# Five pieces for the last weight, and its late sums as two halves of 144 columns in two PSUM banks

## The chip, the cores and the metric

The kernel runs on one core of a Trainium2 chip. The metric is device time in microseconds (us). The kernel before took 215.35 us, the median of three runs (215.19 to 215.35). A core has a matrix engine (PE, with its weight loads shown apart as PEld), a vector engine (DVE), a scalar engine (ACT), a general engine (POOL), a queue engine (SP) and 16 DMA engines. Each engine works through its own list of instructions in order; they meet at semaphores. Matrix products arrive in PSUM (eight banks), from where DVE or ACT copy them to SBUF; DMA moves data between SBUF and the main memory.

## The reference

For four rows `x` of 576 numbers, the output is `x + A + B`, after a first layer norm `xn = layernorm(x)`:

- A is attention over a cache: `q` from `layernorm`ed rows and `wq` (32 heads of 128), keys and values the last 2,048 of 8,192 cached positions of 16 key heads (each serves two query heads), softmax, and the result times `wo` (4096 x 576).
- B is a small mixer: a layer norm, `w1` and a gelu, a shift of four column groups, `w2`, a residual sum, then a layer norm, `w3` (576 x 4608), a gelu and `w4` (4608 x 576).

In short:

```python
xn = layernorm(x)
return x + attention(xn, k_cache[-2048:], v_cache[-2048:], wq) @ wo + mixer(xn, w1, w2, w3, w4)
# the last step inside mixer:  x1 + gelu(layernorm(x1) @ w3) @ w4
```

All inputs and the output are bf16. The output has only 4 rows, so nearly the whole time is spent reading 88.5 MB of cache and weights once.

## The kernel before

Everything that is read comes through one queue, SP's, in a fixed order: `wq`, `w1`, `w2`, `w3`, sixteen pieces of keys (2 MB each), sixteen of values, `wo` in between, and last `w4`. Each operation of every engine is recorded with a sort key by `add` and `add_dma`; an engine's list is its operations sorted by that key, and `waits` names the operations or transfers that must have ended.

The mixer's work up to the gelu behind `w3` is done early, while the keys arrive; its result stands in `h2T_sb` (36 blocks `t` of 128 rows by 4). Then a loop of four rounds transposes keys and makes scores, the softmax follows, and a second loop of four rounds (L429) multiplies the values as they arrive. Then comes the tail that this change is about:

- `pe_turn` and `pe_AO` (L446) multiply the attention result with `wo`, 64 matmuls of 288 columns. `acc_mm` (L444) sends them to four sums `ACC[0..3]`, each of 4 rows and 288 columns: sums 0 and 1 are the two halves of the 576 output columns for even blocks, 2 and 3 the same halves for odd blocks. Sum `k` stands on partitions 32k to 32k+3 and is made by column group `k` of the PE array, so that neighbouring matmuls run side by side. The sums are in banks 0, 1, 2 and 2. Before that, the residual `t1` is put into sums 0 and 1 (`pe_t1`).
- `w4` comes in four pieces given by `W4P`: blocks 0-13, 14-27, 28-33 and 34-35, into the space of the values, so each piece waits for the last loop round that reads that space. The third and the fourth are issued together, after the same wait. The products of blocks 0-13 (`MO0`) go to all four sums.
- The fold: ACT copies sums 2 and 3 from PSUM to SBUF as fp32 (L533), and PE adds them to sums 0 and 1 with two matmuls by a 4 x 4 identity (`pe_fold`, L525).
- Blocks 14-33 (`MO1`, `MO2`) use sums 0 and 1 only, two matmuls of 288 columns per block.
- The last piece is split by output half: the two matmuls of half 0 (`MOl0`), then those of half 1 (`MOl1`). DVE copies half 0 (L550) and ACT copies half 1 (L551), and each half goes out by its own DMA, from SP and from ACT (issued in L177), each waiting for its own copy.

```python
W4P = ((0, 14), (14, 28), (28, 34), (34, 36))
ACC = [ps[32 * k:32 * k + B, min(k, 2), 0:HALF] for k in range(4)]
a = 2 * (t % 2) + h if t < FOLD else h
```

Of the kernel before, what the change touches and what calls it, by code (L numbers as in the profile page):

```python
# [5 lines left out]
FP32 = mybir.dt.float32  # L6
BF16 = mybir.dt.bfloat16
ACTF = mybir.ActivationFunctionType
ALU = mybir.AluOpType
# [10 lines left out]
WO_AFTER = 3  # L20
V0_AFTER = 8
FOLD = 14
W4P = ((0, 14), (14, 28), (28, 34), (34, 36))


class Op:
# [12 lines left out]
def bass_parallel_sum__sliding_block_cached__mixer_s_mlp__decode_kernel(  # L39
    nc, A_x, A_k_cache, A_v_cache, A_wq, A_wo, B_x, B_w1, B_w2, B_w3, B_w4, out  # L40
):
    B, Sq, D = A_x.shape
# [11 lines left out]
    HALF = D // 2  # L54
    FH = F // 2
    RT = F // 128
# [3 lines left out]
    o2 = out.rearrange("b s d -> (b s) d")  # L60

    with ExitStack() as ctx:
        def sb(name, shape, dt):
            return ctx.enter_context(nc.sbuf_tensor(name, shape, dt))
# [43 lines left out]
        h2T_sb = sb("h2T_sb", [128, RT, 32], BF16)  # L108
# [7 lines left out]
        ident_f = sb("ident_f", [128, 128], FP32)  # L116
# [13 lines left out]
        OTx = PTb[:, 1024:1536].rearrange("p (b h q) -> p b h q", b=B, q=4)  # L130
        qmask = sb("qmask", [128, 4], FP32)
        sel32 = sb("sel32", [128, 32], BF16)
        ORT = sb("ORT", [128, 128], BF16)
        t1 = sb("t1", [B, D], FP32)
        fold_sb = P_sb[:, 0:2 * HALF].bitcast(FP32)
        out_t = sb("out_sb", [32 + B, HALF], BF16)
        out_sb = [out_t[32 * h:32 * h + B, :] for h in range(2)]

        ps = ctx.enter_context(nc.psum_tensor("ps", [128, 8, 512], FP32))[:]
        Sps = ps[:, 0:4, :]  # L140
        tb = [ps[:, 4 + k, :].bitcast(BF16).rearrange("p (t d) -> p t d", t=8) for k in range(NTB)]
        ACC = [ps[32 * k:32 * k + B, min(k, 2), 0:HALF] for k in range(4)]
        rinvps = ps[:, 3, 0:128]
        ORps = ps[:, 3, 128:256]
        OTps = lambda g: ps[:, 4 + g % 4, 0:8]
# [20 lines left out]
        def add(engine, emit, waits=(), sig=None, key=0.0, loop=None):  # L166
            seqc[0] += 1
            prog[engine].append(Op(emit, waits, sig, key, seqc[0], loop))

        def add_dma(pairs, skey, waits=(), key=0.0, engine="sp"):  # L170
            if skey not in S:
                S[skey] = sem("s_" + "_".join(str(k) for k in (skey if isinstance(skey, tuple) else (skey,))))
            dma_count[skey] = dma_count.get(skey, 0) + 16 * len(pairs)

            def emit(e):
                for o_, i_ in pairs:
                    e.dma_start(o_, i_).then_inc(S[skey], 16)  # L177
            add(engine, emit, waits, None, key)
            return ("dma", skey, dma_count[skey])
# [6 lines left out]
        KT = KV + G + 8.0  # L186
# [13 lines left out]
        def first_counts(e):  # L200
# [5 lines left out]
          waits=["ident_bf"], sig="perm_k", key=-95.5)  # L206
        P(lambda e: e.tensor_copy(out=perm_p[:].rearrange("p (i b) -> p i b", b=B), in_=ident_bf[:].rearrange("p (b i) -> p i b", b=B)),
          waits=["ident_bf"], sig="perm_p", key=-95)
# [8 lines left out]
        ev_wq, ev_w3, ev_k, ev_v, ev_w4 = [], [], [], [], []  # L217
# [27 lines left out]
        w4_sb = vring_t[:, 0:RT * D].rearrange("p (t n) -> p t n", n=D)  # L245
        for n, (t0, t1_) in enumerate(W4P):
            lst = (t1_ * D - 1) // UE
            ev_w4.append(add_dma([(w4_sb[:, t0:t1_, :], w4_src[:, t0:t1_, :])], ("w4", n),
                                 [f"PV{max(g for g in range(G) if g % NVS == lst)}"], KS + G + 0.1 * n))
        ev_o = [None, None]  # L250
        for h, eng in ((0, "sp"), (1, "act")):
            ev_o[h] = add_dma([(o2[:, HALF * h:HALF * (h + 1)], out_sb[h])], ("out", h),
                              [f"fin{h}"], 10000, engine=eng)
            add(eng, lambda e: None, [ev_o[h]], None, 10001)


# [58 lines left out]
        for j in range(4):  # L315
            add("dve", lambda e, j=j: e.tensor_copy(out=qp_out[:, j, :, :, 0:2], in_=qp_in[:, j, :, 0:B, :]),
                waits=["qTp", "qpad_zero"], sig="qT" if j == 3 else f"qT{j}", key=-25 + 0.1 * j)
# [39 lines left out]
        for n in range(NHB):  # L357
            p = n % 32
# [3 lines left out]
            eng, f = evac(n)  # L362
            add(eng, f, waits=[f"T{n}"] + ([f"SC{n // 8 - 2}"] if n >= 8 else []), sig=("eb", p), key=n + 0.2)
        for g in range(-1, G):
            s_ = g % 4
            if g < G - 1:
                add("pe", pe_SC(g), waits=[("L", ("eb", 8 * s_ + 6), 1), ("L", ("eb", 8 * s_ + 7), 1), ("L", ("qs", s_), 1)], sig=f"SC{g}",
                    key=(g + 1) // 4 + 0.01 * (8 * ((g + 1) % 4) + 1) + 0.005, loop=("k", (g + 1) // 4))
            else:
                add("pe", pe_SC(g), waits=[("c", ("eb", 30), NIT + 1), ("c", ("eb", 31), NIT + 1), ("c", ("qs", 3), NIT + 1)],  # L370
                    sig=f"SC{g}", key=NIT + 0.5)
        for g in range(G):
            P(lambda e, g=g: e.tensor_copy(out=Qs[:, g % 4], in_=Qpad[:, g]), waits=(["qT"] if g == 0 else []) + ([f"SC{g - 4}"] if g >= 3 else []),  # L373
              sig=("qs", g % 4), key=8 * g)
# [4 lines left out]
            waits=["rmax"], sig="negb", key=KS + 0.05)  # L379
        for q in range(4):  # L380
# [3 lines left out]
                waits=["negb"], sig=f"exp{q}", key=KS + 0.1 + 0.01 * q)  # L384
            add("dve", lambda e, cs=cs: e.transpose(PTb[:, cs], P_sb[:, cs]), waits=[f"exp{q}"], sig=f"PTb{q}", key=KS + 0.2 + 0.01 * q)  # L385
            add("pe", lambda e, q=q, cs=cs: e.matmul(ps[:, q, :], lhsT=perm_p[:], rhs=PTb[:, cs], start=True, stop=True),  # L386
                waits=[f"PTb{q}"] + (["perm_p"] if q == 0 else []), sig=f"PTp{q}", key=KS + 0.2 + 0.01 * q)
            dst = PTs[:, 16 * q:16 * q + 16, :].rearrange("p t r -> p (t r)")
            if q % 2 == 1:
                add("act", lambda e, q=q, dst=dst: e.activation(out=dst, in_=ps[:, q, :], func=ACTF.Copy), waits=[f"PTp{q}"],  # L390
                    sig=f"PTs{q}", key=KS + 0.3 + 0.01 * q)
            else:
                add("dve", lambda e, q=q, dst=dst: e.tensor_copy(out=dst, in_=ps[:, q, :]), waits=[f"PTp{q}"],  # L393
                    sig=f"PTs{q}", key=KS + 0.3 + 0.01 * q)
        for g in range(G):
            add("dve", lambda e, g=g: e.tensor_tensor(  # L396
                out=PTg[:, g % NPG], in0=PTs[:, :, 2 * g:2 * g + 2].unsqueeze(2).to_broadcast([128, NT, B, 2]),
                in1=bmask[:].unsqueeze(1).to_broadcast([128, NT, B, 2]), op=ALU.mult),
                waits=[f"PTs{q}" for q in range(4)] + ["bmask"] if g < NPG else [f"PV{g - NPG}"], sig=("pg", g % NPG),
                key=KS + 0.4 + 0.01 * g if g < NPG else KV + g - NPG + 0.6)  # L400
# [3 lines left out]
            waits=["rinv", "ident_f"], sig="diag", key=KS + 0.37)  # L404
        add("dve", lambda e: e.tensor_reduce(out=bmask[:, :, 0], in_=ident_bf[:].rearrange("p (i b) -> p b i", b=B), axis=AX.X, op=ALU.add),
            waits=["ident_bf"], sig="bmask0", key=-41)
        add("dve", lambda e: e.tensor_copy(out=bmask[:, :, 1], in_=bmask[:, :, 0]), waits=["bmask0"], sig="bmask", key=-40.9)
        add("pe", lambda e: e.matmul(rinvps, lhsT=ones_f[:], rhs=diag[:], start=True, stop=True), waits=["diag", "ones_f", "PTs3"],  # L408
            sig="rinvp", key=KS + 0.6)
        add("dve", lambda e: e.tensor_tensor(  # L410
            out=rinvM.rearrange("p b h q -> p (b h) q"),
            in0=rinvps.unsqueeze(2).to_broadcast([128, 128, 4]),
            in1=qmask[:].unsqueeze(1).to_broadcast([128, 128, 4]), op=ALU.mult),
            waits=["rinvp", "qmask"], sig="rinvM", key=KS + 0.6)
        add("dve", lambda e: e.tensor_reduce(out=qmask[:], in_=ident_bf[:].rearrange("p (q r) -> p q r", q=4), axis=AX.X, op=ALU.add),
            waits=["ident_bf"], sig="qmask", key=-40.8)
        add("pool", lambda e: e.tensor_tensor(out=sel32[:], in0=ident_bf[:, 0:32], in1=ident_bf[:, 32:64], op=ALU.add),
            waits=["ident_bf"], sig="sel_a", key=-88)
        add("pool", lambda e: e.tensor_tensor(out=sel32[:], in0=sel32[:], in1=ident_bf[:, 64:96], op=ALU.add),
            waits=["sel_a"], sig="sel_b", key=-87.9)  # L420
        add("pool", lambda e: e.tensor_tensor(out=sel32[:], in0=sel32[:], in1=ident_bf[:, 96:128], op=ALU.add),
            waits=["sel_b"], sig="sel32", key=-87.8)


        def pe_PV(g):
# [7 lines left out]
        for g in range(G):  # L433
# [4 lines left out]
                out=OTx[:, :, 2 * g:2 * g + 2, :], in0=OTps(g).rearrange("p (b e) -> p b e", b=B).unsqueeze(3).to_broadcast([128, B, 2, 4]),  # L438
                in1=rinvM[:, :, 2 * g:2 * g + 2, :], op=ALU.mult),
                waits=["rinvM", f"PV{g}"], sig=("on", m), key=KV + g + 0.5)  # L440


        def acc_mm(e, h, lhsT, rhs, start=False, stop=False, k0=0):
            return e.matmul(ACC[h], lhsT=lhsT, rhs=rhs, start=start, stop=stop, tile_position=(k0, 32 * h))  # L444

        def pe_AO(e):  # L446
            ins = None
            for r in range(32):
                for h in range(2):
                    ins = acc_mm(e, 2 * (r % 2) + h, ORT[:, r:128:32], wo_sb[:, r, HALF * h:HALF * (h + 1)], start=(r == 1))  # L450
            return ins
# [6 lines left out]
        add("dve", lambda e: e.tensor_copy(out=ORT[:], in_=ORps), waits=["turn"], sig="ORT", key=KV + 20)  # L458
        add("pe", pe_AO, waits=["ORT", ev_wo], sig="AO", key=KV + 20)

# [25 lines left out]
        for h in range(2):  # L486
# [3 lines left out]
                waits=[f"hs{h}"], sig="x1" if h else "x1a", key=KH + 0.1 + 0.05 * h)  # L490
# [6 lines left out]
            waits=["hT", "x1nT"], sig="gelu_h", key=KH + 2.1)  # L497
# [24 lines left out]
        add("act", gelu2, waits=["h2_4"], sig="gelu2", key=KW + 0.1)  # L522
        add("dve", lambda e: e.transpose(h2T_sb[:].rearrange("p c i -> p (c i)"), PTb[:, 0:N2]), waits=["gelu2"], sig="h2T", key=KW + 0.2)  # L523

        def pe_fold(e):  # L525
            ins = None
            for h in range(2):
                k0 = 64 + 32 * h
                ins = acc_mm(e, h, ident_f[k0:k0 + B, k0:k0 + B], fold_sb[k0:k0 + B, :], k0=k0)
            return ins  # L530
        n_fold = [z for _, z in W4P].index(FOLD)
        assert FOLD % 2 == 0
        add("act", lambda e: e.activation(out=fold_sb[64:96 + B, :], in_=ps[64:96 + B, 2, 0:HALF], func=ACTF.Copy),  # L533
            waits=[f"MO{n_fold}"], sig="foldc", key=KT + 20 + n_fold + 0.5)
        add("pe", pe_fold, waits=["foldc"], sig="fold", key=KT + 20 + n_fold + 0.5)
        last_p = len(W4P) - 1
        for n, (t0, t1_) in enumerate(W4P):
            def f(e, t0=t0, t1_=t1_, hs=(0, 1)):
                ins = None
                for t in range(t0, t1_):  # L540
                    for h in hs:
                        a = 2 * (t % 2) + h if t < FOLD else h
                        ins = acc_mm(e, a, h2T_sb[:, t, 0:B], w4_sb[:, t, HALF * h:HALF * (h + 1)], stop=(t == RT - 1 or (t == FOLD - 1 and a > 1)))
                return ins
            if n < last_p:
                add("pe", f, waits=[ev_w4[n], "h2T"], sig=f"MO{n}", key=KT + 20 + n)
            else:
                for h in range(2):
                    add("pe", lambda e, f=f, h=h: f(e, hs=(h,)), waits=[ev_w4[n], "h2T"], sig=f"MOl{h}", key=KT + 20 + n + 0.1 * h)
        add("dve", lambda e: e.tensor_copy(out=out_sb[0], in_=ACC[0]), waits=["MOl0"], sig="fin0", key=KT + 50)  # L550
        add("act", lambda e: e.activation(out=out_sb[1], in_=ACC[1], func=ACTF.Copy), waits=["MOl1"], sig="fin1", key=KT + 50)  # L551


        for eng in prog:
# [82 lines left out]
```

## Time and profile before

| what | value |
|---|---|
| median of the runs | 215.35 us (215.19 to 215.35) |
| profiled execution | 215.31 us, of which 214.1 us span from the first to the last instruction |
| DMA | 88.63 MB, mean 414 GB/s |
| PE busy | 139.0 us (65%) |
| DVE busy | 85.2 us (40%) |
| ACT busy | 59.8 us (28%) |
| POOL busy | 10.7 us (5%) |
| mean granted PE clock | 0.785 |

The page divides the span into 40 slices and prints the busy share of each as a digit (9 is 90% or more); PEclk is the clock that PE was granted, in tenths. A group row names line, engine, operation, output and inputs with shapes and count, then busy time and the mean of one, then the idle time before it and what ended it. In a timeline a row is a run of equal instructions: start, length, engine, line, operation, shapes, count, and in brackets the idle time before. The rows shown under the prediction are read in this way.

### The profile page before, as it was taken

The page shows a single profiled execution, that of the slowest core. Times are in us where ns is not written, and L with a number is a line of the kernel's source. Part 1 is how long each engine was busy: PE and PEld are TensorE (multiplying, and loading weights), DVE is VectorE, ACT ScalarE, POOL GpSimd, SP SyncE. Part 2 cuts the span into 40 slices and gives each one's busy share as a digit, 9 for nine tenths or more (in the row PEclk, how much of TensorE's full clock was granted, in tenths as well). Part 3 has the DMA queues.
Part 4 walks back from the last instruction along what each step waited for, and adds up shares of the span by engine and source line. Part 5 has one row for each costly group of instructions (what it writes and reads, how often), then busy time and mean ns, then how long its engine had stood idle before and what let it go on. Part 6 is the DMA issues. An engine that isn't in the chain of part 4 may idle for free.

```text
span 214.1 us, 5690 instructions
## 1 busy us (share of the span) xinstructions
PE 139.0 (65%) x2624; PEld 106.6 (50%) x2624; DVE 85.2 (40%) x162; ACT 59.8 (28%) x72; POOL 10.7 (5%) x37
## 2 busy tenths in 40 slices
PE   0368384999999994999999639433343443333685
PEld 0115132787777884877778406433343433333443
DVE  5502602566666664666666689112111112100000
ACT  2001121466665553566655661000000000000000
POOL 8201000000000100000000000000000000000000
PEclk9999858899999999999999965555555555555579
DMA  6999999999999999999999999999999999999992
GB/s 237 429 403 449 431 414 426 432 421 426 423 432 429 426 429 432 429 426 427 432 429 426 426 442 434 419 416 432 438 416 423 435 432 419 429 435 431 428 404 103
DMA packets 6801, 88.63 MB, mean 414 GB/s; under 512 B 764, under 2 KB 1032, under 8 KB 1800
## 3 DMA queue, kind: packets, MB, share of 16 engines
q1 hardware_dynamic: 6776, 88.50, 97.7%
q8 instruction: 7, 0.11, 0.2%
q14 instruction: 2, 0.02, 0.0%
q10 hardware_dynamic: 16, 0.01, 0.0%
HBM read 88.49 MB, written 0.00 MB: 413 GB/s over the span
## 4 chain that ended last, share of the span: by engine, by line
DMA 52%; PE 36%; DVE 4%; SPq 4%; issue 3%; ACT 0%
DMA vring<-in_A_v_cache_dram 24%; PE ps L335 23%; DMA kring<-in_A_k_cache_dram 21%; PE ps L351 7%; DMA vring<-in_B_w_dram 7%; PE ps L429 5%; SPq L177 4%; DVE PTb L385 1%; DVE rmax L377 1%; DVE regB L343 1%; PE ps L444 1%; DVE PTs L393 1%; PE ps L408 0%; ACT P_sb L382 0%; DVE out_sb L550 0%
## 5 line engine op out<-in xcount | busy, mean ns | idle before, releaser
L343 DVE COPY regB<-ps 128x1024 bf16<-128x1024 bf16 x80 | 52.3, 687 | 33.7 <-PE ps L335 32.1
L335 PE MATMUL ps<-perm_k,kring 128*128 128x128 bf16 x1024 | 61.8, 221 | 5.1 <-DMA kring<-in_A_k_cache_dram 5.0
L335 PEld LDWEIGHTS ps<-perm_k,kring 128*128 128x128 bf16 x1024 | 58.1, 98 | 13.1 <-issue 9.3
L342 ACT ACTIVATE regB<-ps 128x1024 bf16<-128x1024 bf16 x48 | 48.0, 1023 | 40.1 <-PE ps L335 39.9
L429 PE MATMUL ps<-PTg,vring 128*128 128x8 bf16 x1024 | 29.6, 168 | 40.5 <-DMA vring<-in_A_v_cache_dram 34.1
L429 PEld LDWEIGHTS ps<-PTg,vring 128*128 128x128 bf16 x1024 | 28.5, 104 | 41.7 <-DMA vring<-in_A_v_cache_dram 27.6
L437 DVE TENSOR_TENSOR PTb<-ps,PTb 128x32 bf16<-128x32 f32 x16 | 3.1, 192 | 57.8 <-PE ps L429 57.8
L533 ACT ACTIVATE P_sb<-ps 36x288 f32<-36x288 f32 x1 | 0.4, 406 | 77.5 <-PE ps L444 77.5
L351 PE MATMUL ps<-regB,Qs 128*32 128x512 bf16 x272 | 18.3, 389 | 4.2 <-issue 2.7
L351 PEld LDWEIGHTS ps<-regB,Qs 128*32 128x32 bf16 x272 | 6.6, 97 | 10.3 <-issue 5.8
L396 DVE TENSOR_TENSOR PTg<-PTs,bmask 128x512 bf16<-128x512 bf16 x16 | 10.7, 682 | 0.0
L373 POOL COPY Qs<-Qpad 128x128 bf16<-128x128 bf16 x16 | 4.6, 296 | 91.1 <-PE ps L351 79.7
L277 PE MATMUL ps<-ident_bf,xn_bf 4*128 4x4 bf16 x8 | 0.5, 169 | 8.8 <-DVE ragsrc L270 8.8
L299 PE MATMUL ps<-vring,xnT 128*32 128x512 bf16 x40 | 4.6, 629 | 1.9 <-DMA vring<-in_A_wq_dram 1.9
L510 PE MATMUL ps<-regB,x1nT 128*32 128x432 bf16 (+1 forms) x60 | 5.2, 523 | 1.1 <-DMA regB<-in_B_w_dram 0.6
L386 PE MATMUL ps<-PTb,perm_p 128*128 128x512 bf16 x4 | 2.4, 607 | 4.3 <-DVE PTb L385 4.1
L277 PEld LDWEIGHTS ps<-ident_bf,xn_bf 4*128 4x128 bf16 x8 | 0.4, 111 | 8.8 <-POOL ones_f L213 6.3
L444 PE MATMUL ps<-vring,h2T_sb 128*4 128x288 bf16 x72 | 4.2, 298 | 0.7 <-DMA vring<-in_B_w_dram 0.7
L550 DVE CAST out_sb<-ps 4x288 bf16<-4x288 f32 x1 | 0.4, 445 | 10.0 <-PE ps L444 10.0
L444 PE MATMUL ps<-kring,ORT 128*4 128x288 bf16 x64 | 4.0, 443 | 0.4 <-DVE ORT L458 0.4
L523 DVE STREAM_TRANSPOSE h2T_sb<-PTb 128x1152 bf16<-128x1152 bf16 x1 | 1.4, 1378 | 7.2 <-ACT PTb L520 7.2
L263 ACT ACTIVATE sd<-mv 4x1 f32<-4x1 f32 x3 | 0.6, 202 | 12.4 <-DVE mv L261 12.4
(95 smaller groups left out, 68.6 us busy)
## 6 DMA issues: line engine op xcount, KB each, us to landing
kring<-in_A_k_cache_dram SPq DMA_DIRECT2D x16, 2048.0 KB, 16.2
vring<-in_A_v_cache_dram SPq DMA_DIRECT2D x16, 2048.0 KB, 17.6
regB<-in_B_w_dram SPq DMA_DIRECT2D x2, 2304.0 KB, 21.4
kring<-in_A_wo_dram SPq DMA_DIRECT2D x1, 4608.0 KB, 25.1
vring<-in_A_wq_dram SPq DMA_DIRECT2D x2, 2048.0 KB, 9.7
vring<-in_B_w_dram SPq DMA_DIRECT2D x2, 2016.0 KB, 17.4
vring<-in_B_w_dram SPq DMA_DIRECT2D x2, 576.0 KB, 13.8
vring<-in_B_w_dram SPq DMA_DIRECT2D x1, 864.0 KB, 14.7
```

The source lines that it names most:

```text
L177: e.dma_start(o_, i_).then_inc(S[skey], 16)
L299: ins = e.matmul(Qps[32 * j:32 * j + 32, k, :], lhsT=x_, rhs=w, start=(r == 0), stop=(r == 4), tile_position=(0, 32 * j))
L335: ins = e.transpose(tb[n % NTB][:, t, :], kring[:, g % NKS, 8 * k + t, :], perm_k[:])
L342: return "act", lambda e: e.activation(out=ktbuf[:, n % NKT], in_=src, func=ACTF.Copy)
L343: return "dve", lambda e: e.tensor_copy(out=ktbuf[:, n % NKT], in_=src)
L351: ins = e.matmul(Sps[32 * b:32 * b + 32, c4, :].rearrange("p (t i) -> p t i", t=16), lhsT=Qs[:, g % 4, b, :], rhs=kttile[:, t0:t0 + 16, b, :],
L373: P(lambda e, g=g: e.tensor_copy(out=Qs[:, g % 4], in_=Qpad[:, g]), waits=(["qT"] if g == 0 else []) + ([f"SC{g - 4}"] if g >= 3 else []), ...
L396: add("dve", lambda e, g=g: e.tensor_tensor(out=PTg[:, g % NPG], in0=PTs[:, :, 2 * g:2 * g + 2].unsqueeze(2).to_broadcast([128, NT, B, 2]) ...
L429: ins = e.matmul(OTps(g), lhsT=vring[:, g % NVS, t, :], rhs=PTg[:, g % NPG, t].rearrange("p b e -> p (b e)"), start=(t == 0), stop=(t == N ...
L437: add("dve", lambda e, g=g: e.tensor_tensor(out=OTx[:, :, 2 * g:2 * g + 2, :], in0=OTps(g).rearrange("p (b e) -> p b e", b=B).unsqueeze(3) ...
L444: return e.matmul(ACC[h], lhsT=lhsT, rhs=rhs, start=start, stop=stop, tile_position=(k0, 32 * h))
L510: ins = e.matmul(H2ps[k][32 * j:32 * j + 32, :], lhsT=x_, rhs=w, start=(r == 0), stop=(r == 4), tile_position=(0, 32 * j))
```

## The change

- `W4P` gets a fifth piece: blocks 28-32, 33-34, and 35 alone. All three of the late pieces have the same wait as before.
- The four sums of `wo` and blocks 0-13 all stand in bank 0, on the same partitions as before.
- From block 14 on, the sums are four other places, `FIN[h][z]`: half `h` of the output on partitions 32h to 32h+3, and of this half the columns 144z to 144z+143 in bank 1+z. A block has four matmuls of 144 columns instead of two of 288, in the order z = 0 (h = 0, 1), z = 1 (h = 0, 1).
- The fold copies all of the partitions 0 to 99 (36 before, from 64 on), and PE makes the first content of `FIN` from it with four fp32 matmuls by `sel_h`, which adds sums 0 and 2, and 1 and 3. `sel_h` is made by one more POOL instruction near the start of the program.
- The last block is one operation (`MO4`). Then DVE copies bank 1 (36 partitions, 144 columns, both halves of the output) and ACT copies bank 2. Both output DMAs wait for both copies.

```diff
-W4P = ((0, 14), (14, 28), (28, 34), (34, 36))
+W4P = ((0, 14), (14, 28), (28, 33), (33, 35), (35, 36))
...
+        sel_h = sb("sel_h", [128, 2, B], FP32)
...
-        out_sb = [out_t[32 * h:32 * h + B, :] for h in range(2)]
+        OC = HALF // 2
...
-        ACC = [ps[32 * k:32 * k + B, min(k, 2), 0:HALF] for k in range(4)]
+        ACC = [ps[32 * k:32 * k + B, 0, 0:HALF] for k in range(4)]
+        FIN = [[ps[32 * h:32 * h + B, 1 + z, 0:OC] for z in range(2)] for h in range(2)]
...
-            ev_o[h] = add_dma([(o2[:, HALF * h:HALF * (h + 1)], out_sb[h])], ("out", h),
-                              [f"fin{h}"], 10000, engine=eng)
+            ev_o[h] = add_dma([(o2[:, HALF * h:HALF * (h + 1)], out_t[32 * h:32 * h + B, :])], ("out", h),
+                              ["fin0", "fin1"], 10000, engine=eng)
...
+        idh = ident_f[:].rearrange("p (k h c) -> p k h c", k=2, h=2)
+        add("pool", lambda e: e.tensor_tensor(out=sel_h[:], in0=idh[:, 0, :, 0:B], in1=idh[:, 1, :, 0:B], op=ALU.add),
+            waits=["ident_f"], sig="sel_h", key=-87.7)
...
+        def fin_mm(e, h, z, lhsT, rhs, start=False, stop=False):
+            return e.matmul(FIN[h][z], lhsT=lhsT, rhs=rhs, start=start, stop=stop, tile_position=(0, 32 * h))
+
         def pe_fold(e):
             ins = None
-            for h in range(2):
-                k0 = 64 + 32 * h
-                ins = acc_mm(e, h, ident_f[k0:k0 + B, k0:k0 + B], fold_sb[k0:k0 + B, :], k0=k0)
+            for z in range(2):
+                for h in range(2):
+                    ins = fin_mm(e, h, z, sel_h[0:96 + B, h, :], fold_sb[0:96 + B, OC * z:OC * (z + 1)], start=True)
             return ins
...
-        add("act", lambda e: e.activation(out=fold_sb[64:96 + B, :], in_=ps[64:96 + B, 2, 0:HALF], func=ACTF.Copy),
+        add("act", lambda e: e.activation(out=fold_sb[0:96 + B, :], in_=ps[0:96 + B, 0, 0:HALF], func=ACTF.Copy),
...
                 for t in range(t0, t1_):
-                    for h in hs:
-                        a = 2 * (t % 2) + h if t < FOLD else h
-                        ins = acc_mm(e, a, h2T_sb[:, t, 0:B], w4_sb[:, t, HALF * h:HALF * (h + 1)], stop=(t == RT - 1 or (t == FOLD - 1 and a > 1)))
+                    for i in range(4 if t >= FOLD else 2):
+                        z, h = i // 2, i % 2
+                        lhsT, c0 = h2T_sb[:, t, 0:B], HALF * h + OC * z
+                        if t < FOLD:
+                            ins = acc_mm(e, 2 * (t % 2) + h, lhsT, w4_sb[:, t, c0:c0 + HALF], stop=(t >= FOLD - 2))
+                        else:
+                            ins = fin_mm(e, h, z, lhsT, w4_sb[:, t, c0:c0 + OC], stop=(t == RT - 1))
                 return ins
-            if n < last_p:
-                add("pe", f, waits=[ev_w4[n], "h2T"], sig=f"MO{n}", key=KT + 20 + n)
-            else:
-                for h in range(2):
-                    add("pe", lambda e, f=f, h=h: f(e, hs=(h,)), waits=[ev_w4[n], "h2T"], sig=f"MOl{h}", key=KT + 20 + n + 0.1 * h)
-        add("dve", lambda e: e.tensor_copy(out=out_sb[0], in_=ACC[0]), waits=["MOl0"], sig="fin0", key=KT + 50)
-        add("act", lambda e: e.activation(out=out_sb[1], in_=ACC[1], func=ACTF.Copy), waits=["MOl1"], sig="fin1", key=KT + 50)
+            add("pe", f, waits=[ev_w4[n], "h2T"], sig=f"MO{n}", key=KT + 20 + n)
+        add("dve", lambda e: e.tensor_copy(out=out_t[0:32 + B, 0:OC], in_=ps[0:32 + B, 1, 0:OC]), waits=[f"MO{last_p}"], sig="fin0", key=KT + 50)
+        add("act", lambda e: e.activation(out=out_t[0:32 + B, OC:HALF], in_=ps[0:32 + B, 2, 0:OC], func=ACTF.Copy),
+            waits=[f"MO{last_p}"], sig="fin1", key=KT + 50)
```

More of the change, by code (lines that the diff above doesn't have):

```diff
@@ L532, in bass_parallel_sum__sliding_block_cached__mixer_s_mlp__decode_kernel @@
         assert FOLD % 2 == 0
-        add("act", lambda e: e.activation(out=fold_sb[64:96 + B, :], in_=ps[64:96 + B, 2, 0:HALF], func=ACTF.Copy),
+        add("act", lambda e: e.activation(out=fold_sb[0:96 + B, :], in_=ps[0:96 + B, 0, 0:HALF], func=ACTF.Copy),
             waits=[f"MO{n_fold}"], sig="foldc", key=KT + 20 + n_fold + 0.5)
-        add("pe", pe_fold, waits=["foldc"], sig="fold", key=KT + 20 + n_fold + 0.5)
+        add("pe", pe_fold, waits=["foldc", "sel_h"], sig="fold", key=KT + 20 + n_fold + 0.5)
@@ L536, in bass_parallel_sum__sliding_block_cached__mixer_s_mlp__decode_kernel, with f @@
         last_p = len(W4P) - 1
         for n, (t0, t1_) in enumerate(W4P):
-            def f(e, t0=t0, t1_=t1_, hs=(0, 1)):
+            def f(e, t0=t0, t1_=t1_):
                 ins = None
                 for t in range(t0, t1_):
-                    for h in hs:
-                        a = 2 * (t % 2) + h if t < FOLD else h
-                        ins = acc_mm(e, a, h2T_sb[:, t, 0:B], w4_sb[:, t, HALF * h:HALF * (h + 1)], stop=(t == RT - 1 or (t == FOLD - 1 and a > 1)))
-                return ins
```

## The prediction

> **What bounds the kernel now.** I read the page first, then the chain that ended last, then the timeline of the last eight microseconds, because the change touches nothing earlier but one small POOL instruction. The page's slices (40 of 5.35 us) show the DMA engines full from the second slice to the last but one and PE never the bound:
>
> ```profile
> span 214.1 us, 5690 instructions
> ...
> PEclk9999858899999999999999965555555555555579
> DMA  6999999999999999999999999999999999999992
> ...
> q8 instruction: 7, 0.11, 0.2%
> ```
>
> The chain from 190 us on (start, length, what) is transfers until 210.88, and then for the first time compute:
>
> ```profile
> 176.61 17.64 DMA vring<-in_A_v_cache_dram
> ...
> 196.19 14.69 DMA vring<-in_B_w_dram
> 210.88 0.04 issue
> 210.92 1.20 PE ps L444 x16
> 212.12 0.43 DVE out_sb L550
> ```
>
> So only what follows the last weights can be shortened by compute, and what precedes them only by moving fewer or earlier bytes. The timeline of that tail (start, length, engine, line, idle before):
>
> ```profile
> 207.25 0.41 ACT L533 ACTIVATE P_sb<-ps 36x288 f32<-36x288 f32 x1 [77.50 <-PE ps L444]
> ...
> 207.71 0.65 PE L444 MATMUL ps<-P_sb,ident_f 4*4 4x288 f32 x4 [0.52 <-ACT P_sb L533]
> ...
> 208.84 1.88 PE L444 MATMUL ps<-vring,h2T_sb 128*4 128x288 bf16 x28 [0.49 <-DMA vring<-in_B_w_dram]
> ...
> 210.92 1.15 PE L444 MATMUL ps<-vring,h2T_sb 128*4 128x288 bf16 x16 [0.20 <-DMA vring<-in_B_w_dram]
> ...
> 211.62 0.12 PEld L444 LDWEIGHTS ps<-vring,h2T_sb 128*4 128x4 bf16 x4
> 212.10 0.45 DVE L550 CAST out_sb<-ps 4x288 bf16<-4x288 f32 x1 [9.97 <-PE ps L444]
> 212.14 0.40 ACT L551 ACTIVATE out_sb<-ps 4x288 bf16<-4x288 f32 x1 [4.49 <-PE ps L444]
> 212.57 0.35 SPq L177 DMA_DIRECT2D out_dram<-out_sb  x1
> ```
>
> The row at 210.92 holds two pieces, 12 matmuls of blocks 28 to 33 and 4 of blocks 34 and 35. The four weight loads at 211.62 are those of the last piece. PE answered a landing 0.04 us later (210.88 to 210.92 in the chain), so the last piece landed at about 211.58 and the piece before the big one at 208.80. From 211.58 to the output's issue at 212.57 pass 0.99 us; from there to the end of the span 1.53 us, which the change doesn't touch.
>
> **Part 1, five pieces instead of four.** The bytes are the same. SP's issues, of the two last pieces and of two early transfers of short packets (start, length):
>
> ```profile
> 3.28 0.48 SPq L177 DMA_DIRECT2D vring<-in_B_w_dram  x1
> ...
> 3.80 0.48 SPq L177 DMA_DIRECT2D vring<-in_B_w_dram  x1
> ...
> 196.19 0.33 SPq L177 DMA_DIRECT2D vring<-in_B_w_dram  x1
> ...
> 196.56 0.43 SPq L177 DMA_DIRECT2D vring<-in_B_w_dram  x1
> ```
>
> The same four in the list of DMA issues, in the same order (KB, us from issue to landing):
>
> ```profile
> vring<-in_B_w_dram SPq DMA_DIRECT2D x1, 576.0 KB, 14.1
> ...
> vring<-in_B_w_dram SPq DMA_DIRECT2D x1, 72.0 KB, 13.9
> ...
> vring<-in_B_w_dram SPq DMA_DIRECT2D x1, 864.0 KB, 14.7
> ...
> vring<-in_B_w_dram SPq DMA_DIRECT2D x1, 288.0 KB, 15.0
> ```
>
> 864 KB took 208.80 to 210.88 = 2.08 us, 288 KB took 0.70 us. A straight line through both gives 2.4 ns per KB and 0.01 us fixed: the lower end of what one more piece costs. The upper end: the 72 KB (128 packets of 576 B) landed at 17.70, 0.32 us after the 576 KB at 17.38; its bytes are worth 0.17, so 0.15 us is fixed, 0.25 with the rows' rounding. The new last piece has packets of 1,152 B, between the two. I take 0.09 us: last landing 211.67 (211.59 to 211.83). The pieces before it then land at about 210.53 (720 KB: 1.73 us after 208.80) and, the last 144 KB taking 0.35 us and its fixed 0.09, at 211.23.
> SP issues one more DMA behind 196.56, some 0.4 us. What is queued behind it is the output's issue, for which SP waits 15 us anyway; it costs nothing, and 0.4 us if that wait were gone.
>
> **Part 2, the matmuls of blocks 14 to 35 in two halves of 144 columns.** Their 44 matmuls become 88, their loads too. The two column groups run side by side: 28 matmuls in 1.88 us with one lasting 286 ns are 14 pairs at (1.88 - 0.286) / 13 = 123 ns. The price of a short matmul, from these rows (minimum, median and maximum in ns; then a stretch of a stream of 128 columns with one load each):
>
> ```profile
> L444 PEld LDWEIGHTS ps<-vring,h2T_sb x44: 80/85/85, 208.8 to 211.7; 128*4 128x4 bf16 x44
> L444 PE MATMUL ps<-vring,h2T_sb x44: 284/286/286, 208.8 to 211.8; 128*4 128x288 bf16 x44
> L335 PE MATMUL ps<-perm_k,kring x260: 216/219/229, 59.8 to 80.0; 128*128 128x128 bf16 x130
> L335 PEld LDWEIGHTS ps<-perm_k,kring x258: 95/98/98, 59.9 to 80.0; 128*128 128x128 bf16 x129
> ...
> 59.81 1.67 PE L335 MATMUL ps<-perm_k,kring 128*128 128x128 bf16 x27
> ```
>
> The stream runs at (1.67 - 0.219) / 26 = 56 ns. Between 56 ns at 128 columns and 123 at 288, 144 columns come to 62.5 ns; between 219 and 286, one matmul lasts 226 ns. The 14 blocks from 208.84 then issue until 208.84 + 27 x 0.0625 = 210.53, as now; five blocks end their issue at 211.2, and the two that land at 211.23 at 211.5, before the last piece's landing. So PE stays hidden until 211.67, starts at 211.71, issues the second pair at 211.77 and ends at 212.00. It ended now at 212.10 - 0.03 = 212.07 (DVE's start less the signal): 0.07 us gained. Bounds from the rows: the pair rate no better than 56 ns, no worse than the load's 85 ns (the rival below).
>
> **Part 3, the copies.** Each engine takes 144 columns of both column groups (36 partitions) instead of 288 columns of one. Rows of copies out of PSUM:
>
> ```profile
> L458 DVE CAST ORT<-ps 128x128 bf16<-128x128 f32 x1 | 0.3, 292 | 0.6 <-PE ps L455 0.6
> L550 DVE CAST out_sb<-ps 4x288 bf16<-4x288 f32 x1 | 0.4, 445 | 10.0 <-PE ps L444 10.0
> L390 ACT ACTIVATE PTs<-ps 128x512 bf16<-128x512 f32 x2 | 1.2, 597 | 0.8 <-PE ps L386 0.7
> L551 ACT ACTIVATE out_sb<-ps 4x288 bf16<-4x288 f32 x1 | 0.4, 402 | 4.5 <-PE ps L444 4.5
> L533 ACT ACTIVATE P_sb<-ps 36x288 f32<-36x288 f32 x1 | 0.4, 406 | 77.5 <-PE ps L444 77.5
> ```
>
> 36 partitions cost what 4 do (406 against 402). DVE: (445 - 292) / 160 = 0.96 ns per column, so 307 ns; ACT: (597 - 402) / 224 = 0.87, so 277 ns. DVE ends at 212.00 + 0.03 + 0.31 = 212.34, ACT, which starts 0.04 later, at 212.35. That is 0.20 us before the 212.55 of now, of which 0.07 is the matmuls'. If no part of a copy were fixed, DVE would need 222 ns: 0.09 more.
>
> **Part 4, two waits per output DMA.** SP and ACT each wait for both copies instead of one. The copies end together, so no time is added but a second wait instruction; no row prices it. Bounds: nothing, and the 0.04 us that PE needs from a landing to its start. I take 0.02: issue at 212.40 against 212.57.
>
> **What I cost at nothing.** The fold: ACT's copy has the same columns; four products of 144 columns stand for two of 288, and the x4 of its row says each is made in two passes, so again four side-by-side steps' worth, 0.65 us. It ends at 208.36 and the weights are awaited until 208.80: 0.44 us of cover, beyond which each 0.1 us costs 0.1 on PE, which from there has only about 0.2 to spare. The four sums of blocks 0 to 13 move into one bank (now three): the sums of groups 2 and 3 already share one. One POOL instruction comes behind
>
> ```profile
> 6.77 0.24 POOL L421 TENSOR_TENSOR sel<-sel,ident_bf 128x32 bf16<-128x32 bf16 x1
> 18.43 0.77 POOL L373 COPY Qs<-Qpad 128x128 bf16<-128x128 bf16 x3 [11.42 <-DVE Qpad L316]
> ```
>
> with 11 us free behind it; at 0.24 us it would be paid only if that wait vanished.
>
> **Sum.** +0.09 landing, -0.16 from last landing to PE's end (0.49 to 0.33), -0.13 copies, +0.02 wait: about -0.17 us. The profiled execution took 215.31 us, 214.1 of it span; the median of the runs is 215.35. So 215.35 - 0.17 = 215.2 us. Own range: landing -0.08 to +0.16, copies -0.09, wait -0.02 to +0.02: 215.0 to 215.4, all within 0.2% (0.43 us), about what a measurement of this kernel can tell from no change.
>
> **Rivals.** First, on the other side: PE becomes the bound because 60 ns of matmul no longer cover a weight load. The loads last 80 to 85 ns, 288 columns cover that, 144 don't. For it: no row shows a short matmul in column groups at full clock. Against it: the 128-column stream runs at 56 ns though its loads last 98. Should a pair need 85 ns, the last matmul ends at 208.84 + 43 x 0.085 + 0.226 = 212.72, 0.72 late: 215.9 us. The gain is gone from 72 ns per pair, and beyond 82 ns it is slower by more than 0.2%.
> The Trainium skill bears on this: "TensorE: Matmul & The Clock Gate", section "Back-to-back issue gap", gives about 81 ns per matmul for a stream of load and matmul at 128 columns, which by the formula above would be 215.7 us. The trace disagrees with it at 56 ns. The same page, section "The mechanism" of its part on tiling, says a load overlaps running matmuls only in another row group; here all share one, yet pairs follow at 123 ns where 120 is streaming, so the trace disagrees again.
>
> Second: an instruction fetch falls badly. The seven fetches took 0.2% of 16 engines' span, 0.2% x 16 x 214.1 / 7 = 1 us each. PE's code behind the loop grows by 46 matmuls and as many loads. If that brings one more fetch onto a DMA engine that lands last, or PE waits for one, up to 1 us: 216.2, and 215.8 for half. Against it: seven fetches served the whole program, whose execution shows 5,690 instructions; 92 more ask for a fraction of one.
>
> Third, faster by more than I say: the last landing is set by the engines furthest behind. This row of stretches (length, PE, PEld, DVE, ACT, POOL, clock, DMA share, GB/s)
>
> ```profile
> 208.84:210.92 2.08, 1.88 (x28) 1.15 (x29) 0.00 (x0) 0.00 (x0) 0.00 (x0) 1.00 0.56 219
> ```
>
> says that nearly half of the engines' time is idle there. If the other cut of the pieces lets the laggards finish 0.2 us sooner than now (0.29 less than in the sum), with the copies at their lower bound: 215.35 - 0.17 - 0.29 - 0.09 = 214.8 us. Nothing in the change evens them out, but nothing holds their lag fixed either.
>
> **Chances.** The forecast (215.0 to 215.4) 0.55; the third rival 0.20; the load-bound PE 0.15; the fetch 0.10. The first is "same", the third "faster", the other two "slower". The range reaches to 214.85 and to 216.0: it leaves out about half of the third rival and of the fetch.
>
> **What would show it.** Right: last landing near 211.67, pairs at 62 ns, last matmul lasting 226 ns, copies of about 307 and 277 ns, output issue near 212.40. Wrong: pairs at 72 ns or more with PE busy without a gap from 208.8, an eighth q8 packet, a last landing off by more than 0.2 us, or a clock below 1.00 after 206.4.

## The result and the profile after

The changed kernel takes 215.06 us, the median of 22 runs (214.92 to 215.35), against 215.30 us for 22 runs of the kernel before (215.19 to 216.57). The ratio is 0.9985, with a 95% interval of 0.9979 to 0.9992: 0.32 us faster, between 0.17 and 0.45. By the medians it is 0.24 us; one run of the kernel before, at 216.57 us, lies far above its other 21. Both gains are under 0.2% (0.43 us).

The profiled execution of the changed kernel took 215.35 us, the slowest of its 22, with a span of 214.0. Its totals therefore say nothing against the 215.31 of before; the tail, counted from a common event, does. The chain that ended last (start, length, what):

```profile
191.50 17.49 DMA vring<-in_B_w_dram
208.99 0.04 issue
209.03 3.11 PE ps L531 x88
212.14 0.02 issue
212.17 0.30 DVE out_sb L558
```

Blocks 14 to 27 landed at 208.99 here and at 208.80 before, so this execution is 0.19 us late before the changed part begins. From there PE is on the chain without a gap that the chain counts, where before it stood behind a transfer until 210.92. The timeline from 211.70 on (one of the 12 matmuls of the last two pieces had ended by then and isn't counted):

```profile
211.48 0.65 PE L531 MATMUL ps<-vring,h2T_sb 128*4 128x144 bf16 x11
211.83 0.09 PEld L531 LDWEIGHTS ps<-vring,h2T_sb 128*4 128x4 bf16 x4
212.16 0.28 ACT L559 ACTIVATE out_sb<-ps 36x144 bf16<-36x144 f32 x1 [4.63 <-PE ps L531]
212.17 0.30 DVE L558 CAST out_sb<-ps 36x144 bf16<-36x144 f32 x1 [9.83 <-PE ps L531]
212.53 0.28 ACTq L179 DMA_DIRECT2D out_dram<-out_sb  x1
212.54 0.35 SPq L179 DMA_DIRECT2D out_dram<-out_sb  x1
```

The four loads at 211.83 are those of the last block. By the 0.04 us of the chain the last piece landed at 211.79. PE ended 0.03 us before DVE's start, at 212.13; the copies ended at 212.47. Read in the same way, the two executions compare so:

| stretch, us | before | after | difference |
|---|---|---|---|
| landing of block 27 to the last landing | 2.78 | 2.80 | +0.02 |
| last landing to PE's end | 0.49 | 0.34 | -0.15 |
| PE's end to the end of the copies | 0.48 | 0.34 | -0.14 |
| copies to the output's issue | 0.03 | 0.07 | +0.04 |
| sum | 3.78 | 3.55 | -0.23 |

The sum agrees with the 0.24 us between the medians. The groups behind it, copies first, then the matmuls and their loads (minimum, median, maximum in ns):

```profile
L541 ACT ACTIVATE P_sb<-ps 100x288 f32<-100x288 f32 x1 | 0.4, 410 | 75.8 <-PE ps L449 75.8
L558 DVE CAST out_sb<-ps 36x144 bf16<-36x144 f32 x1 | 0.3, 300 | 9.8 <-PE ps L531 9.8
L559 ACT ACTIVATE out_sb<-ps 36x144 bf16<-36x144 f32 x1 | 0.3, 283 | 4.6 <-PE ps L531 4.6
```

```profile
L531 PEld LDWEIGHTS ps<-vring,h2T_sb x88: 80/85/85, 209.0 to 211.8; 128*4 128x4 bf16 x88
L531 PE MATMUL ps<-vring,h2T_sb x88: 224/226/226, 209.0 to 211.9; 128*4 128x144 bf16 x88
```

A matmul of 144 columns lasts 226 ns, a load still 85. The timeline of PE from the start of block 14, cut at 211 us:

```profile
209.03 2.17 PE L531 MATMUL ps<-vring,h2T_sb 128*4 128x144 bf16 x64 [0.78 <-DMA vring<-in_B_w_dram]
```

The 64 matmuls are 32 pairs, so a pair takes (2.17 - 0.226) / 31 = 62.7 ns. Blocks 14 to 32 are 38 pairs and end their issue at 209.03 + 38 x 0.0627 = 211.41; the next piece starts at 211.48 and needs until 211.73; the last starts at 211.83. PE waits 0.07 and 0.10 us for the last two pieces: it is close to being the bound, but is not.

### The profile page after: what moved, and what is told of

It reads as the page before. It is cut to its first block, busy times and chain, and to the rows that moved or that the text cites. A ratio compares the mean times of both kernels' runs of the same rounds, so it can differ in the third digit from the quotient of the medians.

```text
span 214.0 us, 5789 instructions
## 1 busy us (share of the span) xinstructions
PE 139.3 (65%) x2670; PEld 108.2 (51%) x2672; DVE 85.1 (40%) x162; ACT 59.3 (28%) x72; POOL 10.8 (5%) x38
## 4 chain that ended last, share of the span: by engine, by line
DMA 52%; PE 36%; DVE 4%; SPq 4%; issue 2%; ACT 0%
DMA vring<-in_A_v_cache_dram 23%; PE ps L337 23%; DMA kring<-in_A_k_cache_dram 21%; DMA vring<-in_B_w_dram 8%; PE ps L353 7%; PE ps L434 4%; SPq L179 4%; PE ps L531 1%; DVE PTb L387 1%; DVE rmax L379 1%; DVE regB L345 1%; DVE PTs L395 1%; PE ps L410 0%; ACT P_sb L384 0%; DVE out_sb L558 0%
## 5 line engine op out<-in xcount | busy, mean ns | idle before, releaser
L337 PEld LDWEIGHTS ps<-perm_k,kring 128*128 128x128 bf16 x1024 | 58.9, 99 | 11.9 <-issue 8.6
L353 PE MATMUL ps<-regB,Qs 128*32 128x512 bf16 x272 | 18.8, 397 | 4.6 <-issue 3.5
L388 PE MATMUL ps<-PTb,perm_p 128*128 128x512 bf16 x3 | 1.8, 609 | 4.9 <-DVE PTb L387 4.8
L515 PEld LDWEIGHTS ps<-regB,x1nT 128*32 128x32 bf16 x60 | 2.0, 132 | 4.8 <-DMA regB<-in_B_w_dram 2.7
```

Of the source, the lines that this page charges most:

```text
L337: ins = e.transpose(tb[n % NTB][:, t, :], kring[:, g % NKS, 8 * k + t, :], perm_k[:])
L353: ins = e.matmul(Sps[32 * b:32 * b + 32, c4, :].rearrange("p (t i) -> p t i", t=16), lhsT=Qs[:, g % 4, b, :], rhs=kttile[:, t0:t0 + 16, b, :],
L515: ins = e.matmul(H2ps[k][32 * j:32 * j + 32, :], lhsT=x_, rhs=w, start=(r == 0), stop=(r == 4), tile_position=(0, 32 * j))
```

## Experiments

Each comparison below is with the kernel before in the same group of runs. The medians of the changed kernel itself come out alike when it is measured again beside the others, so differences of 0.1 us between medians can be read and differences of 0.03 us can't.

### The changed kernel again

No edit.

> The changed kernel once more, as the measure for the others of this group. From its first trace: last landing to PE's end 0.33 us against 0.49 before, copies 0.34 against 0.48, one more wait 0.04, one more piece 0.02: 0.24 us under the kernel before. A theory in which the transfers themselves end sooner says instead that the last landing is earlier against the landing of block 27 (2.78 us before).

> The changed kernel, measured beside the four-group version: 0.24 us under the kernel before, give or take 0.1.

215.02 us against 215.28 (12 and 35 runs; ratio 0.9984, 0.9974 to 0.9994), and 215.08 against 215.34 (11 and 22 runs; 0.9985, 0.9974 to 0.9995): 0.26 us faster both times. From block 27's landing to the last landing the two traces have 2.86 and 2.80 us. So the transfers do not end sooner than before, and the theory that the gain is theirs has nothing to stand on in the landings.

### One part at a time: the pieces alone, the halves alone

The pieces alone, on the kernel before:

```diff
-W4P = ((0, 14), (14, 28), (28, 34), (34, 36))
+W4P = ((0, 14), (14, 28), (28, 33), (33, 35), (35, 36))
```

> The kernel before with five pieces alone. My theory: after the last landing PE has two matmuls of 288 columns side by side, 0.04 + 0.29 = 0.33 us instead of 0.49; the copies stay at 0.48; the extra piece costs 0.02 (its price in the trace of the change) to 0.09 (my prediction): 0.07 to 0.14 us under the kernel before. Rival, that the gain is the transfers' (the other cut lets the DMA engines that lag finish sooner): the whole gain of the change, 0.24 or more.

The halves alone, on the changed kernel:

```diff
-W4P = ((0, 14), (14, 28), (28, 33), (33, 35), (35, 36))
+W4P = ((0, 14), (14, 28), (28, 34), (34, 36))
```

> The changed kernel with the four old pieces: only the two banks of 144 columns and the shared copies. My theory: last landing to PE's end 0.45 us (eight matmuls, four steps of 62 ns and 226 ns) against 0.49, copies 0.34 against 0.48, second wait +0.04: 0.10 to 0.15 us under the kernel before. Rival, that the gain is the transfers': no gain, 0.0.

The pieces alone take 215.15 us, 0.13 under the kernel before; the halves alone 215.18, 0.10 under it (ratios 0.9996, 0.9981 to 1.0012, and 0.9989, 0.9975 to 1.0003). Each interval alone reaches to no change; the two medians add up to 0.23, against 0.26 for the changed kernel of this group. By the ratios the parts are 0.09 and 0.24, so the run times alone don't tell how the gain is divided, nor exclude that it is all the pieces'. What divides it here are the tails, one trace of each. The pieces alone:

```profile
211.57 0.08 PEld L444 LDWEIGHTS ps<-vring,h2T_sb 128*4 128x4 bf16 x2 [0.26 <-DMA vring<-in_B_w_dram]
211.90 0.45 DVE L550 CAST out_sb<-ps 4x288 bf16<-4x288 f32 x1 [9.80 <-PE ps L444]
211.93 0.40 ACT L551 ACTIVATE out_sb<-ps 4x288 bf16<-4x288 f32 x1 [3.96 <-PE ps L444]
212.36 0.28 ACTq L177 DMA_DIRECT2D out_dram<-out_sb  x1
```

Landing at 211.53, PE's end at 211.87: 0.34 instead of 0.49, the old copies at their old 0.45 and 0.40, issue 0.83 us after the landing where before it was 0.99. From block 27's landing (208.75) to the last pass 2.78 us, as before. The halves alone:

```profile
210.86 1.17 PE L531 MATMUL ps<-vring,h2T_sb 128*4 128x144 bf16 x32 [0.20 <-DMA vring<-in_B_w_dram]
...
211.42 0.40 PEld L531 LDWEIGHTS ps<-vring,h2T_sb 128*4 128x4 bf16 x12
212.07 0.28 ACT L559 ACTIVATE out_sb<-ps 36x144 bf16<-36x144 f32 x1 [4.95 <-PE ps L531]
212.07 0.30 DVE L558 CAST out_sb<-ps 36x144 bf16<-36x144 f32 x1 [10.01 <-PE ps L531]
212.43 0.28 ACTq L179 DMA_DIRECT2D out_dram<-out_sb  x1
```

Here loads run on through the last landing: PE is still at the six blocks of the piece before when the last one comes, so its end, 212.04, comes 0.5 us after the landing (211.5, by the issue and the time to landing of its 288 KB), no earlier than in the kernel before. The 0.45 us that was expected here left out that PE is still busy when the piece lands. Only the copies gain. So the pieces give the matmuls' 0.15 us and the halves give the copies' 0.14 less 0.04 for the second wait; neither touches the transfers. The rival in which the transfers gain wanted all of it with the pieces and none with the halves.

### What a piece costs

```diff
-W4P = ((0, 14), (14, 28), (28, 33), (33, 35), (35, 36))
+W4P = ((0, 14), (14, 28), (28, 30), (30, 32), (32, 33), (33, 34), (34, 35), (35, 36))
```

> The changed kernel with eight pieces instead of five (28-29, 30-31, then 32, 33, 34, 35 alone), which prices a piece. My prediction's 0.09 us per piece: last landing 0.27 us later against that of block 27, and 0.27 over the changed kernel. The 0.02 of its trace: 0.06 over it. If the cut itself evens out the lagging engines, it is under the changed kernel.

215.19 us: 0.09 under the kernel before (0.9989, 0.9975 to 1.0003) and 0.17 over the changed kernel of the same group, 0.06 us for each of three more pieces. The trace agrees:

```profile
208.64 3.28 PE L531 MATMUL ps<-vring,h2T_sb 128*4 128x144 bf16 x88 [0.89 <-DMA vring<-in_B_w_dram]
211.63 0.09 PEld L531 LDWEIGHTS ps<-vring,h2T_sb 128*4 128x4 bf16 x4 [0.30 <-DMA vring<-in_B_w_dram]
```

From block 27's landing to the last 2.99 us, 0.19 more than the 2.80 of the changed kernel. My 0.09 per piece and the 0.02 read from one trace were both off, on either side; that a finer cut evens out the lagging engines is out, since the time rose. The fifth piece alone costs less than the next three: nine traces of kernels with five pieces have 2.78 to 2.86 us there, with a median of 2.80, and the three with four pieces 2.78, 2.80 and 2.81. Why the first is free was not settled.

### What hides a weight load

The rival against the change was that 60 ns of matmul can't cover an 85 ns load. Quarters of 72 columns in four banks put the question harder:

```diff
-        OC = HALF // 2
+        OC = HALF // 4
...
-        FIN = [[ps[32 * h:32 * h + B, 1 + z, 0:OC] for z in range(2)] for h in range(2)]
+        FIN = [[ps[32 * h:32 * h + B, 1 + z, 0:OC] for z in range(4)] for h in range(2)]
...
-                    for i in range(4 if t >= FOLD else 2):
+                    for i in range(8 if t >= FOLD else 2):
```

The fold loops over four quarters as well, and each copy takes two banks.

> The changed kernel with quarters of 72 columns in four banks: four steps per block instead of two, each copy takes two banks of 72. It asks what hides a weight load. If matmuls stream (72 / 2.4 + 2.5 ns a pair): 32.5 ns a pair, 130 ns a block, no change of time against the changed kernel. If a pair cannot go under the load's 85 ns: 340 ns a block, 22 blocks take 7.5 us instead of 2.75, about 4.5 us slower. If there is a floor per instruction in between (27 ns a matmul, as the 8-column stream of the values shows at half clock): 54 ns a pair, 216 ns a block, 4.8 us for 22 blocks, about 1.9 us slower.

216.07 us, 0.73 over the kernel before (1.0036, 1.0023 to 1.0049) and about 1.0 over the changed kernel: none of the three values that I had worked out. The timeline of PE and its loads, then one matmul and one load (minimum, median, maximum in ns):

```profile
208.78 1.85 PEld L531 LDWEIGHTS ps<-vring,h2T_sb 128*4 128x4 bf16 x112 [0.79 <-DMA vring<-in_B_w_dram]
208.79 1.98 PE L531 MATMUL ps<-vring,h2T_sb 128*4 128x72 bf16 x111 [0.59 <-DMA vring<-in_B_w_dram]
211.52 1.23 PE L531 MATMUL ps<-vring,h2T_sb 128*4 128x72 bf16 x65 [0.75 <-issue]
```

```profile
L531 PEld LDWEIGHTS ps<-vring,h2T_sb x176: 80/88/88, 208.8 to 212.5; 128*4 128x4 bf16 x176
L531 PE MATMUL ps<-vring,h2T_sb x176: 193/198/198, 208.8 to 212.6; 128*4 128x72 bf16 x176
```

The second row holds 55 pairs and the first matmul of the next: (1.98 - 0.198) / 55 = 32.4 ns a pair, the rate of the first of the three values. Loads of 88 ns, of four weight columns each, are hidden behind matmuls that start every 32 ns. The rival is out, not only for 144 columns. But then PE stood still for 0.75 us, before the 112th matmul, the last of blocks 14 to 27, with no wait shown ("issue"): its weights had been loaded (112 loads), its data had landed at 208.75. In its place a new question: what was PE waiting for?

### What PE stood still for

The page of the quarters counts one fetch of instructions (queue q8) more than the pages of the kernels before and after. A fetch is about 0.13 MB / 8 = 16 KB. The next kernel moves PE's program against these blocks, and does nothing else: 30 small matmuls of zeros near the start, where PE is idle.

```diff
+        def pe_pad(e):
+            ins = None
+            for _ in range(30):
+                ins = e.matmul(ps[:, 7, 0:8], lhsT=zeros_bf[:, 0:128], rhs=zeros_bf[:, 0:8], start=True, stop=True)
+            return ins
+        add("pe", pe_pad, waits=["zeros_bf"], sig="pad", key=-50)
```

> The quarters of 72 columns again, with 30 small matmuls (8 columns, zeros, into an unused bank) near the start of PE's program, where PE is idle. They do nothing but move all later instructions by 60 places. The quarters' trace has PE stand still for 0.95 us in the middle of blocks 14 to 27, with no wait shown. If that is PE's instruction fetch (a 16 KB block is asked for when PE enters the block before it, and 256 quick instructions use that one up first), the shift lets PE enter it in the slow part before the fold, the standstill goes, and the time falls by about 1.0 us to that of the changed kernel. If it is a wait for data, a semaphore or a bank, the standstill stays where it is: 0.7 us over the kernel before.

> The control: the changed kernel with the same 30 small matmuls. By either theory no change against the changed kernel (0.24 us under the kernel before, give or take 0.1), as long as the moved blocks don't stall the loops.

The moved quarters take 215.07 us against 215.26 (0.9983, 0.9967 to 0.9998): 0.19 us under the kernel before, where unmoved they were 0.73 over it, so 0.9 us less, and level with the changed kernel. The changed kernel with the same matmuls takes 215.09 against 215.26 (0.9991, 0.9976 to 1.0007), 0.17 under the kernel before, within what was expected of it. The tail of the moved quarters has no standstill:

```profile
208.36 0.67 PE L537 MATMUL ps<-P_sb,sel_h 100*4 100x72 f32 x16 [0.52 <-ACT P_sb L547]
208.89 3.09 PE L537 MATMUL ps<-vring,h2T_sb 128*4 128x72 bf16 x176
```

The number of fetches is the same, eight, by the pages of the two:

```profile
q8 instruction: 8, 0.13, 0.3%
```

```profile
q8 instruction: 8, 0.13, 0.2%
```

What differs is when the last two run. In the quarters none runs between 206 and 208.9, and this line of the DMA queues is that of 208.9 to 209.5:

```profile
q8 instruction: 1, 0.02, 10.9%
```

In the moved quarters the same line appears between 206 and 208:

```profile
q8 instruction: 1, 0.02, 3.4%
```

In narrower windows the packets of the last two fetches begin at 209.08 and 212.63 in the quarters, at 207.29 and 210.89 in the moved quarters; they last 1.0 to 1.2 us. In the changed kernel the same 30 matmuls move the last fetch from 209.24 to 207.22.

That the standstill hangs on the place in the program, and not on data, a semaphore or a bank, is shown: 60 places near the start were added and nothing else, and in the changed kernel they alone gave no gain. That the cause is a fetch is not shown. For it speaks that these fetches move with PE's program. But no packet of a fetch runs during the standstill: the nearest ended at 210.13, PE stopped at 210.77 and went on at 211.52. A fetch near 209 also stands in the traces of the kernels before (208.82) and after (209.24), where PE stood still for nothing of the kind, and in the moved quarters one begins at 210.89, in the middle of the stream, without harm. What links the fetch and the standstill, if anything does, is not seen in these traces.

### Four column groups

If two steps of 62 ns remain after the last landing, four column groups make them one:

```diff
-        FIN = [[ps[32 * h:32 * h + B, 1 + z, 0:OC] for z in range(2)] for h in range(2)]
+        FIN = [[ps[64 * z + 32 * h:64 * z + 32 * h + B, 1 + z, 0:OC] for z in range(2)] for h in range(2)]
...
-            return e.matmul(FIN[h][z], lhsT=lhsT, rhs=rhs, start=start, stop=stop, tile_position=(0, 32 * h))
+            return e.matmul(FIN[h][z], lhsT=lhsT, rhs=rhs, start=start, stop=stop, tile_position=(0, 64 * z + 32 * h))
...
-        add("act", lambda e: e.activation(out=out_t[0:32 + B, OC:HALF], in_=ps[0:32 + B, 2, 0:OC], func=ACTF.Copy),
+        add("act", lambda e: e.activation(out=out_t[0:32 + B, OC:HALF], in_=ps[64:96 + B, 2, 0:OC], func=ACTF.Copy),
```

> The changed kernel with the four quarters of the output (2 x 144 columns of each half) on four column groups instead of two groups and two banks one after the other; ACT copies from partitions 64 to 99. My theory of the tail: the four matmuls of the last block run side by side, 0.04 + 0.23 = 0.27 us after the landing instead of 0.33, so 0.06 us under the changed kernel. If PE's near-full stream of 2.75 us for 22 blocks was binding in the median run, the block rate of 62 ns instead of 125 frees more: 0.1 to 0.2 us. Otherwise no change.

> The four-group version again, beside the other three: 0.25 to 0.35 us under the kernel before.

215.01 us against 215.34 (0.9988, 0.9979 to 0.9997), where the changed kernel had 215.08 beside it; and 214.99 against 215.26 (0.9982, 0.9971 to 0.9994). That is 0.33 and 0.27 us under the kernel before, and 0.07 under the changed kernel, which is about what the tail gives:

```profile
211.56 0.23 PE L531 MATMUL ps<-vring,h2T_sb 128*4 128x144 bf16 x4
211.85 0.30 DVE L558 CAST out_sb<-ps 36x144 bf16<-36x144 f32 x1 [9.78 <-PE ps L531]
211.85 0.29 ACT L559 ACTIVATE out_sb<-ps 36x144 bf16<-36x144 f32 x1 [4.68 <-PE ps L531]
```

The four last matmuls start together; PE ends at 211.79, 0.27 us after the landing at 211.52, instead of 0.34. More than this was not to be had, so PE's nearly full stream did not bind the changed kernel. It has the lowest medians of all kernels here; the intervals of it and of the changed kernel overlap.

The same with the four old pieces (`W4P` as in the kernel before):

> The four-group version with the four old pieces of w4. It weighs a piece against a block: two steps instead of one after the last landing, 0.06 us more, against one piece less, by 0.02 to 0.06 us. Equal to the four-group version within 0.05 us.

215.05 us against 215.26 (0.9986, 0.9975 to 0.9998), 0.06 over the four groups with five pieces beside it: equal within what can be read, and no gain from saving a piece. Its trace has something else in it. These rows of stretches give PE's granted clock as the last but two number, first for this kernel, then for the four groups with five pieces:

```profile
207.60:211.03 3.43, 1.81 (x83) 1.09 (x79) 0.00 (x0) 0.41 (x1) 0.00 (x0) 1.00 0.68 271
211.03:212.10 1.07, 0.97 (x32) 0.47 (x24) 0.05 (x1) 0.05 (x1) 0.00 (x0) 0.50 0.01 2
```

```profile
207.60:211.03 3.43, 1.58 (x80) 1.13 (x76) 0.00 (x0) 0.00 (x0) 0.00 (x0) 1.00 0.69 271
211.03:212.10 1.07, 0.53 (x12) 0.19 (x12) 0.25 (x1) 0.25 (x1) 0.00 (x0) 1.00 0.01 2
```

In this execution the last piece ran at half clock, after a PE that was busy for 1.81 of the 3.43 us before. That alone doesn't explain it: with five pieces PE was busy for only 1.58 us of the same stretch and kept its clock of 1.00. Why the clock fell stays open. How often that happens in its other runs is not known; the median gives no sign of it.

## Why the prediction was right, point by point

The time was forecast at 215.2 us and came out at 215.06; the gain at 0.17 and is 0.24 by the medians, 0.32 by the ratio. The range, 215.0 to 215.4, takes in the 215.30 of the kernel before as well, so the time alone would have borne it out with no gain at all; what speaks for the forecast is its terms. The mechanism is the forecast one: the tails of the kernels with one part alone show the shorter matmuls with the pieces and the shorter copies with the halves. The four terms as printed in the sum add up to 0.18; the measured ones are:

- **Landing.** Forecast 0.09 us later, measured 0.02 in the first trace and no difference over all traces of five and of four pieces. This is the term of the sum that was mis-sized most, and it explains the gain that was missing. The lower end, 0.01, from the straight line through two late pieces, was the right row; the early transfers of 576-byte packets were the wrong neighbour. Three more pieces do cost 0.06 each.
- **Matmuls.** Last landing to PE's end: forecast 0.33, measured 0.34. The matmul of 144 columns was put at 226 ns and lasts 226; the step at 62.5 and is 62.7.
- **Copies.** DVE was put at 307 ns and took 300, ACT at 277 and took 283. The straight lines through the other copies were good to 2%. ACT was expected to start 0.04 us after DVE, as in the row before, and started 0.01 before it; the copies' end is DVE's.
- **Second wait.** Forecast 0.02 us, measured 0.04, the upper bound that had been given. That it is the second wait fits the pieces alone: there each DMA waits for one copy, and the issue follows the copies as closely as in the kernel before.
- **Costed at nothing.** The fold's copy of 100 partitions takes 410 ns against 406 for 36, and PE waited 0.78 us for the data behind the fold: the cover held. The DMA issue, the POOL instruction and the one bank for four sums leave nothing in the tail.
- **First rival, PE bound by its loads.** Out: a pair takes 63 ns at 144 columns and 32 at 72. The two places of the Trainium skill that were weighed against the trace, in "TensorE: Matmul & The Clock Gate", sections "Back-to-back issue gap" and "The mechanism", are not borne out by these runs either: the first has no such figure for 72 columns, but four loads and matmuls of that width take 65 ns in all here, and loads overlap matmuls in the same row group. The prediction read the second section too narrowly, though: by the Trainium skill a load may also go ahead of running matmuls into "the background weight buffer", and that these runs do not contradict.
- **Second rival, an instruction fetch.** It did not come in the changed kernel (its page counts seven fetches, as before). The quarters show a standstill that hangs on the place in the program, at 0.75 us, and about 0.9 us of time, close to the price that was given; that a fetch causes it is argued, not shown. The argument against the rival, that 92 more instructions ask for a fraction of a fetch, was right in its result and weak as an argument: the moved quarters have as many fetches as the unmoved and don't stand still.
- **Third rival, transfers that end sooner.** Out by the landings.

## What to carry to other kernels

In the tail behind the last transfer, count from the last landing: what must still be loaded, multiplied, copied and issued is a sum of short durations that other rows of the same trace price to a few per cent. Make the last piece small, and let every engine that can copy take an equal share of the columns, since 100 partitions cost no more than 36 here (410 ns against 406); a small extra piece here cost nothing, three more cost 0.06 us each. Where straight-line PE code becomes much denser, look for standstills without a wait: the one found here came from where the code lies, and moving it by 60 instructions told.

## What the runs showed of the hardware that was not expected

- Matmuls of 72 columns on two column groups, each with its own 88 ns load of four weight columns, start every 32.4 ns per pair: the loads are hidden completely.
- A dense stream of PE instructions stood still for 0.75 us with no wait shown, and 60 instructions inserted some 200 us earlier removed that; the run time fell by 0.9 us. The 16 KB fetches of instructions moved with them, the last two from 209.08 and 212.63 to 207.29 and 210.89; whether they cause the standstill is open.
- The first additional piece at the end of a long queue cost nothing that nine traces could show, the next three 0.06 us each.
